# State updates and scores of spans 6 to 10 on quarters of the array, and another issue order for spans 0 to 9

## The chip, the cores and the metric

The kernel runs on one core of a Trainium2 chip. The metric is device time in microseconds (us) of one execution. The core has TensorE (PE in the profile; its weight loads are listed apart as PEld), VectorE (DVE), ScalarE (ACT), GpSimd (POOL) and SyncE (SP), which here only issues DMAs. Each engine works through its own queue in order and waits for others by semaphores.

## The reference, cut to what matters

A gated linear recurrence per head, then a feed-forward layer with ELU:

```python
def _attn_ref(q, k, v, alpha):            # (4, 8, 768, 48) each
    for t in range(S):
        state = alpha[:, :, t, :, None] * state + einsum('bhd,bhe->bhde', k[:, :, t], v[:, :, t])
        y[:, :, t] = einsum('bhd,bhde->bhe', q[:, :, t], state)
...
def _moe_ref(x, w_in, w_out):             # x: 3072 x 384, w_in: 384 x 2048, w_out: 2048 x 384
    h = x @ w_in
    g = where(h > 0, h, exp(minimum(h, 0)) - 1)
    return g @ w_out
```

x is y with the heads side by side. The result is wanted in near float32 accuracy, so each operand of the large products is split into a high and a low fp32r part and three products are summed.

## The kernel before

**Recurrence.** The sequence of each of the four batches is cut into six spans (the code's windows) of 128 steps, 24 in all, numbered i; a span has two chunks of 64 steps. Eight heads lie on the partitions in two halves (48 rows of each 64), four times along the free axis. A span passes these steps, each named by one or two letters in the code:

- L (LA, LB): load of q, k and alpha; LV: load of v in its two layouts into one of four buffers vs. V0 (lines 181 to 183) loads for spans 6 to 9 a second copy of the first half of v, whose other half stays zero.
- SC: running product P of alpha (L192). LN, EX, KA, KB, KC: the decay factors and the scaled k (L201 to L224). SQ: q times P into the tile st (L235, L238); ZS (L245) zeroes the other half of st for spans 6 to 10.
- TP and KN: transposes of k by PE and a copy by ACT, in spans 0 to 5; TA and TB: 32 by 32 transposes by DVE, from span 6 on.
- S: scores on PE; MK: their mask on DVE (L335, L330).
- U: products of k and v on PE; UA, UB, UC (L381, L410, L412): the states after each chunk. UP corrects U of span 1 on PE.
- YL, Y3 and Y: output of the span on PE; XH and XL: its high and low part in x; XP: the low part on PE for spans 0 and 1; XD: a small DMA that brings heads 6 and 7 to their rows of x.

S and U come in two forms. Before span QS (scores) or QU (updates), S (L318) and U (L362) use all 128 rows of the array, against zeros in one half, and 64 or 48 of its columns, and write one PSUM bank. From there on, S4 (L303) and U4 (L346) go round the four 64 by 64 quarters of the array:

```python
QU, QS, SHARE = 10, 11, 11
...
    QUADS = ((0, 0), (1, 1), (0, 1), (1, 0))
...
            for a, c in QUADS:
                r, cs = slice(64 * a, 64 * a + D), slice(c * C, (c + 1) * C)
```

and write two banks; from span SHARE on, the scores of a span use the banks that the updates of the span before left. Both forms have 16 matmuls (32 passes, as they are float32). The mask in the first form is two DVE instructions of 64 x 512, in the second four of 64 x 256 (QUADS again).

**Feed-forward.** x is worked in 12 blocks of 256 tokens (b), d_ff in 8 groups of 256 (j). A.b.j: h from x and w_in, 18 matmuls (L625); RA, RB, RC: the ELU on ACT, ACT and DVE; GH and GL: its high and low part (ACT, DVE); O.b.j: 12 matmuls into two PSUM banks (L676); Z.b: store.

**Weights.** They come as pairs of 32-bit words and are rebuilt on the chip: F loads one of 16 pieces, DA, DB, DC (DVE, L551 to L563) rebuild two pieces at a time, WH (ACT, L589) makes the high part, WL (L609) the low part, on DVE for the pieces in WLV and on POOL for the others. WP makes the low parts of pieces 0 and 2 on PE. KAV, KBV and SQV say in the same way for which spans KA, KB and SQ run on DVE rather than on POOL.

**Order.** START lists the steps of spans 0 to 9 and of the first 25 A.b.j, with the weights, in the order of issue; each engine gets its instructions in that order. After it, a loop (`steady`) places the steps by fixed distances. PSUM has eight banks under one tag; a new tile takes a bank that was released earlier in the program. X.2 in START are two matmuls on constants whose result nobody reads, and 12 of them (WARM) stand ahead of it.

Of the kernel before, what the change touches and what calls it, by code (L numbers as in the profile page):

```python
# [42 lines left out]


START = """
LA.0 SC.0 X.2 LB.0 LN.0 EX.0 LA.1 SQ.0 LB.1 KA.0 KB.0 SC.1 SQ.1 F.0 F.2 KC.0 LN.1 EX.1 LV.1 KA.1 LV.0 S.0 KB.1
TP.0 KC.1 L.2 PC.0 TP.1 KN.1 KN.0 L.3 PC.1 DA.0 DB.0 S.1 DC.0 U.0 WH.0 U.1 UC.0 X.2 UA.0 UP.1 SC.2 WP.0 F.6
WH.2 LN.2 SQ.2 MK.1 F.4 LV.3 F.1 UC.1 SC.3 UA.1 EX.2 MK.0 WP.2 DA.2 F.3 YL.1 KA.2 L.5 YL.0 LV.2 KB.2 KC.2 F.9
LN.3 Y3.1 Y.1 EX.3 DB.2 Y3.0 KA.3 PC.2 KB.3 Y.0 WL.0 XH.1 LC.0 S.2 F.11 TP.2 XP.1 XH.0 KN.2 XP.0 SQ.3 KC.3
DC.2 TP.3 DA.1 U.2 XL.1 KN.3 U.3 DB.1 WL.2 DC.1 WH.4 UB.2 XL.0 F.5 S.3 L.4 PC.3 A.0.0 UA.2 WH.6 WH.1 UC.2 F.10  # L50
A.0.1 CA.0 WL.6 A.0.3 MK.2 UB.3 UA.3 WH.3 MK.3 UC.3 WL.4 RA.0.0 YL.2 F.7 LV.5 RB.0.0 YL.3 RA.0.1 Y3.2 SC.4
WL.1 Y3.3 F.12 SC.5 SQ.4 DA.3 WL.3 LN.5 Y.2 LN.4 RB.0.1 SQ.5 F.8 Y.3 RC.0.0 EX.4 EX.5 F.14 A.0.2 RC.0.1 XH.3
XH.2 L.7 XL.3 XL.2 GH.0.0 GH.0.1 KA.4 GL.0.0 DA.5 DB.3 KA.5 KB.5 DC.3 CB.0 LV.7 V0.7 LV.6 V0.6 RA.0.2 RA.0.3
A.1.0 RB.0.2 LV.4 UB.6 A.1.3 KC.5 A.1.1 RC.0.2 GL.0.1 TP.5 RB.0.3 WH.7 RA.1.3 GH.0.2 RC.0.3 S.5 DA.4 RA.1.0
RB.1.3 WL.7 GL.0.2 WH.5 KN.5 DB.5 A.1.2 RB.1.0 O.0.0 MK.5 RC.1.3 DB.4 GH.0.3 WL.5 O.0.1 RA.1.2 O.0.2 LC.1
RC.1.0 KB.4 GL.0.3 L.6 RA.1.1 KC.4 DC.4 TP.4 RB.1.1 KN.4 DC.5 GH.1.0 WH.8 GL.1.0 O.0.3 U.4 GH.1.3 PC.5 GL.1.3
WL.8 RB.1.2 RC.1.1 WH.11 GH.1.1 DA.6 GL.1.1 S.4 A.0.4 RC.1.2 O.1.0 WH.10 MK.4 DB.6 GH.1.2 GL.1.2 RA.0.4 WL.11
PC.4 UB.4 WL.10 O.1.1 RB.0.4 WH.9 DC.6 O.1.2 A.0.5 WL.9 WH.12 U.5 F.15 UC.4 UB.1 UA.4 F.13 RC.0.4 Y.4 UA.5
WH.14 RA.0.5 GH.0.4 RB.0.5 GL.0.4 WL.12 CA.1 SC.6 LN.6 SC.7 WL.14 O.1.3 RC.0.5 DA.7 A.0.7 L.8 A.0.6 LN.7 DB.7
GH.0.5 RA.0.7 GL.0.5 DC.7 EX.6 KA.6 XH.4 O.0.4 RB.0.7 XL.4 RA.0.6 WH.13 RB.0.6 WL.13 A.1.4 RC.0.7 A.1.5 O.0.5  # L60
EX.7 WH.15 KB.6 GH.0.7 KA.7 RC.0.6 KB.7 GH.0.6 RA.1.4 GL.0.7 UB.0 RA.1.5 LV.8 Y.5 GL.0.6 A.1.6 CB.1 KC.6
RB.1.5 XD.4 WL.15 RB.1.4 XH.5 O.0.6 TB.6 RC.1.5 SQ.6 ZS.6 ZV.6 O.0.7 SQ.7 ZS.7 RA.1.6 RC.1.4 GH.1.4 XL.5
GH.1.5 GL.1.4 RB.1.6 XD.5 TA.6 GL.1.5 A.2.3 Z.0 RA.2.3 RC.1.6 U.6 V0.8 KC.7 GH.1.6 S.6 S.7 TA.7 RB.2.3 RC.2.3
O.1.4 GL.1.6 A.1.7 A.2.4 LC.2 MK.6 PC.6 A.2.2 UA.6 UC.6 SC.8 RA.1.7 RB.1.7 TB.7 GH.2.3 LN.8 O.1.5 Y.6 EX.8
RC.1.7 SQ.8 ZS.8 KA.8 GH.1.7 L.10 MK.7 RA.2.2 U.7 KB.8 GL.1.7 O.1.6 RB.2.2 A.2.0 KC.8 LV.9 V0.9 UB.7 UC.7 PC.7
TA.8 UA.7 L.9 RC.2.2 XH.6 LV.10 RA.2.0 RB.2.0 O.1.7 RC.2.0 A.2.1 Z.1 SC.9 GH.2.0 RA.2.1 TB.8 XL.6 A.2.7 RA.2.4
GL.2.0 RB.2.1 Y.7 GL.2.3 RC.2.1 LN.9 U.8 RB.2.4 GH.2.2 EX.9 S.8 MK.8 SQ.9 ZS.9 XH.7 A.2.6 XD.6 XL.7 O.2.0
RA.2.7 KA.9 RB.2.7 GH.2.1 GL.2.2 RC.2.4 A.2.5 RC.2.7 UB.8 GL.2.1 PC.8 RA.2.6 RB.2.6 UC.8 O.2.1 RA.2.5 SC.10
UA.8 KB.9 XD.7 RB.2.5 O.2.2 LN.10 A.3.0 O.2.3 GH.2.4 LV.11 RC.2.5 RC.2.6 GH.2.7 L.11 KC.9 RA.3.0 TB.9 EX.10
GH.2.5 RB.3.0 GL.2.4 O.2.4 KA.10 SQ.10 ZS.10 KB.10 GH.2.6 GL.2.5 KC.10 GL.2.7 GL.2.6 TA.9 RC.3.0 O.2.5 TB.10  # L70
TA.10 O.2.6 PC.9 S.9 GH.3.0 MK.9 GL.3.0
"""
# [896 lines left out]
```

## Time and profile before

| | us |
|---|---|
| median of 3 runs | 513.34 (511.15 to 514.16) |
| profiled execution | 510.82 |
| its span | 509.1 |
| outside the span | 1.7 |
| busy: PE | 499.0 (98%) |
| busy: DVE | 394.3 (77%) |
| busy: ACT | 301.5 (59%) |
| busy: POOL | 123.2 (24%) |

Busy is the time in which an engine had an instruction running; idle time of an engine is listed with what ended it. The timeline merges instructions of one line in a row: start, busy time, line, shapes and how many. Matmuls overlap, so the duration of a group runs a little past the start of the next; from the start of one group to that of the next is what the group took on PE. The scan of SC is printed as TENSOR_TENSOR_SCAN in the trace and as SCALAR_TENSOR_TENSOR in listings of the order.

### The profile page before, as it was taken

To read this page: it belongs to the slowest core of one execution; us is meant where nothing else is said; L and a number is where in the kernel's file an instruction comes from. 1 tells how busy PE (TensorE), PEld (TensorE's weight loads), DVE (VectorE), ACT (ScalarE), POOL (GpSimd) and SP (SyncE) were. 2 spreads that over 40 slices of the span, in tenths; PEclk is the share of its full clock that TensorE was granted. 3 is DMA by queue.
4 is the path that set the end of the run, shared out by engine and by line. 5 is a ranking of instruction groups with operands and counts; after the bars stand their busy time and mean duration, and the time that the engine had idled before them with its cause. 6 is when DMAs were issued, how large, how long until landed. Compare 5 with 4: busy or idle time off the path is not lost.

```text
span 509.1 us, 13170 instructions
## 1 busy us (share of the span) xinstructions
PE 499.0 (98%) x5404; PEld 482.5 (95%) x5404; DVE 394.3 (77%) x801; ACT 301.5 (59%) x689; POOL 123.2 (24%) x115
## 2 busy tenths in 40 slices
PE   6999999999999999999999999999999999999996
PEld 3789999999999999999999999999999999999995
DVE  7898998998999788788888888788888887333431
ACT  3576566644653657667667667666666665564442
POOL 3233631643420304303303304303213110000000
PEclk9999999999999999999999999999999999999999
DMA  8999605032330442432532523524524221210001
GB/s 311 403 410 382 188 1 215 13 120 76 119 102 1 133 148 54 158 121 77 164 102 94 165 79 117 164 72 124 160 74 127 71 66 37 72 40 1 31 4 36
DMA packets 22724, 61.53 MB, mean 121 GB/s; under 512 B 2944, under 2 KB 10112, under 8 KB 22656
## 3 DMA queue, kind: packets, MB, share of 16 engines
q1 hardware_dynamic: 22368, 60.22, 36.0%
q8 instruction: 44, 0.72, 0.6%
q10 hardware_dynamic: 288, 0.39, 0.2%
q14 instruction: 24, 0.20, 0.1%
HBM read 53.92 MB, written 4.72 MB: 115 GB/s over the span
## 4 chain that ended last, share of the span: by engine, by line
PE 95%; DMA 3%; SPq 1%; issue 1%; DVE 0%; ACT 0%
PE h L625 41%; PE o L676 40%; PE y L428 4%; DMA vs<-in_vv_dram 3%; PE sc L318 2%; PE q L346 2%; PE u L362 1%; PE y L423 1%; PE q L303 1%; PE wp L112 1%; PE tp L259 0%; SPq L535 0%; PE y L467 0%; PE yl L423 0%; SPq L174 0%
## 5 line engine op out<-in xcount | busy, mean ns | idle before, releaser
L625 PE MATMUL h<-xt,w 128*128 128x256 f32 x1728 | 221.4, 282 | 0.0
L625 PEld LDWEIGHTS h<-xt,w 128*128 128x128 f32 x1728 | 214.0, 188 | 1.5
L676 PE MATMUL o<-w,gh 128*128 128x384 f32 x768 | 198.4, 339 | 0.0
L676 PEld LDWEIGHTS o<-w,gh 128*128 128x128 f32 x768 | 135.6, 188 | 0.2
L676 PE MATMUL o<-w,gl 128*128 128x384 f32 x384 | 129.9, 338 | 0.0
L649 ACT CAST gh<-h 128x512 fp32r<-128x512 f32 x96 | 56.3, 587 | 88.3 <-DVE h L643 71.7
L643 DVE SCALAR_TENSOR_TENSOR h<-r,h 128x512 f32<-128x512 f32 x96 | 66.1, 693 | 51.1 <-ACT r L638 50.5
L633 ACT ACTIVATE r<-h 128x512 f32<-128x512 f32 x96 | 56.7, 594 | 75.1 <-PE h L625 73.5
L238 POOL TENSOR_TENSOR st<-qka,P 64x512 f32<-64x512 f32 x36 | 42.9, 1190 | 212.0 <-issue 166.5
L662 DVE TENSOR_TENSOR gl<-h,gh 128x512 fp32r<-128x512 f32 x96 | 66.1, 690 | 34.2 <-ACT gh L649 33.0
L269 DVE STREAM_TRANSPOSE kn<-qka 32x128 f32<-32x128 f32 x288 | 87.1, 302 | 4.1
L676 PEld LDWEIGHTS o<-w,gl 128*128 128x128 f32 x384 | 72.1, 188 | 0.0
L638 ACT ACTIVATE r<-r 128x512 f32<-128x512 f32 x96 | 60.5, 633 | 2.5
L192 DVE TENSOR_TENSOR_SCAN P<-qka,first 128x516 f32<-128x516 f32 x24 | 29.6, 1237 | 2.3 <-DMA qka<-in_qka_dram 1.5
L214 POOL TENSOR_TENSOR qka<-qka,R 128x512 f32<-128x512 f32 x18 | 23.9, 1330 | 12.5 <-ACT R L206 12.4
L219 POOL TENSOR_TENSOR R<-P,R 128x512 f32<-128x512 f32 x19 | 24.7, 1300 | 5.0 <-DVE qka L214 3.9
L330 DVE TENSOR_TENSOR st<-q,mask 64x256 f32<-64x256 f32 x52 | 22.0, 422 | 1.0
L428 PEld LDWEIGHTS y<-st,vs 128*64 128x64 f32 x576 | 18.3, 138 | 4.2 <-issue 4.0
L581 ACT ACTIVATE ck<-ck,lim 128x384 f32<-128x384 f32 x32 | 20.9, 653 | 1.0
L428 PE MATMUL y<-st,vs 128*64 128x64 f32 x576 | 20.7, 225 | 0.0
L201 ACT ACTIVATE R<-P 128x512 f32<-128x512 f32 x24 | 15.1, 633 | 8.4 <-DVE P L192 8.4
L576 ACT ACTIVATE ck<-ck 128x384 f32<-128x384 f32 x32 | 18.2, 568 | 0.1
(105 smaller groups left out, 418.5 us busy)
## 6 DMA issues: line engine op xcount, KB each, us to landing
qka<-in_qka_dram SPq DMA_DIRECT2D x22, 770.0 KB, 5.1
raw<-in_wgt_dram SPq DMA_DIRECT2D x16, 768.0 KB, 11.2
ck<-in_wgt_dram SPq DMA_DIRECT2D x32, 384.0 KB, 3.1
vs<-in_vv_dram SPq DMA_DIRECT2D x36, 192.0 KB, 5.3
out_dram<-ot SPq DMA_DIRECT2D x22, 192.0 KB, 2.0
vs<-in_vv_dram SPq DMA_DIRECT2D x6, 384.0 KB, 9.3
xt<-y SPq DMA_DIRECT2D x40, 48.0 KB, 2.3
qka<-in_qka_dram SPq DMA_DIRECT2D x2, 512.0 KB, 4.8
```

Of the source, the lines that this page charges most:

```text
L192: nc.vector.tensor_tensor_scan(out=P.rearrange("p n w -> p (n w)"), data0=t[:, 2 * NP * W:], data1=first.rearrange("p n w -> p (n w)"), in ...
L219: eng(KBV, i).tensor_tensor(out=d["R"], in0=pw(i), in1=d["R"], op=ALU.mult)
L238: eng(SQV, i).tensor_tensor(out=st[r, a], in0=d["q"][r], in1=pw(i)[r], op=ALU.mult)
L269: nc.vector.transpose(out=kn[32 * t:32 * t + 32, :, 32 * g:32 * g + 32], in_=d["kt"][32 * g:32 * g + 32, :, 32 * t:32 * t + 32])
L428: nc.tensor.matmul(out[64 * a:64 * a + m], lhsT=lhs(i, c, a)[:, n * D:n * D + m], rhs=d["st"][:, a, n, c * C:(c + 1) * C], start=start, st ...
L625: nc.tensor.matmul(h[:, f, :], lhsT=t[:, wi, ws], rhs=x[:, c, xi, :], start=(f == 0 and k == 0), stop=(k == 8), skip_group_check=True)
L633: nc.scalar.activation(out=r, in_=d["h"], func=AF.Relu, scale=-1.0)
L638: nc.scalar.activation(out=d["r"], in_=d["r"], func=AF.Exp, scale=-1.0)
L643: nc.vector.scalar_tensor_tensor(out=d["h"], in0=d["r"], scalar=-1.0, in1=d["h"], op0=ALU.add, op1=ALU.max)
L649: nc.scalar.copy(out=gh, in_=d["h"])
L662: nc.vector.tensor_tensor(out=gl, in0=d["h"], in1=d["gh"].bitcast(F32), op=ALU.subtract)
L676: nc.tensor.matmul(o[:, 0:DM], lhsT=gt[:, f, ms], rhs=t[:, wi, f * DM:f * DM + DM], start=(j == 0 and f == 0 and k == 0), stop=(j == NJ - ...
```

## The change

QU and QS go to 6, so that spans 6 to 10 use the quarters as well (updates of 6 to 9, scores of 6 to 10). With this V0 and ZS do nothing and are no longer in START, UB and UC of span 6 take the form of the later spans, and each U and each S of these spans holds two banks rather than one (SHARE stays 11). The lists that say what runs on DVE change, and START is another order. The steady part changes only in U of span 9, S of span 10, and what hangs on them.

```diff
-QU, QS, SHARE = 10, 11, 11
+QU, QS, SHARE = 6, 6, 11
 
-WLV, KAV, KBV, SQV = (1, 3, 9, 10, 12), (0, 1, 3, 6, 7, 10), (0, 1, 2, 3, 8), (1, 3, 4, 5)
+WLV, KAV, KBV, SQV = (0, 4), (0, 1, 2, 3, 10), (0, 3, 5, 6), (1, 2, 3, 5)
...
-LA.0 SC.0 X.2 LB.0 LN.0 EX.0 LA.1 SQ.0 LB.1 KA.0 KB.0 SC.1 SQ.1 F.0 F.2 KC.0 LN.1 EX.1 LV.1 KA.1 LV.0 S.0 KB.1
...
+LA.0 LB.0 SC.0 LN.0 EX.0 LA.1 KA.0 KB.0 LB.1 SC.1 X.2 LV.0 LN.1 X.2 KC.0 F.2 SQ.0 EX.1 F.0 TP.0 KN.0 S.0 U.0
...
```

What the first lines move on PE, from the last matmul on constants ahead of the first span: wp is the constants' bank, sc the scores, tp the transposes, u the updates, yl and y the outputs, wd the weights' low part. Before:

```order
L112 MATMUL wp<-first 128x512
L318 MATMUL sc<-st,qka 64x64 x16
L259 MATMUL tp<-ident,qka 128x128 x8
L318 MATMUL sc<-st,qka 64x64 x16
L362 MATMUL u<-vs_105,kn 64x48 x16
L362 MATMUL u<-vs_106,kn 64x48 x16
L112 LDWEIGHTS first
L112 MATMUL wp<-first 128x512
L112 LDWEIGHTS first
L112 MATMUL wp<-first 128x512
L388 MATMUL u<-vs_106,minus 128x192 x2
L598 MATMUL wd<-wm,ident 128x384
```

After, on PE, the same place (all line numbers are one lower):

```order
L111 MATMUL wp<-first 128x512
L258 MATMUL tp<-ident,qka 128x128 x4
L317 MATMUL sc<-st,qka 64x64 x16
L361 MATMUL u<-vs_105,kn 64x48 x16
L422 MATMUL yl<-st,vs_105 64x64 x6
L258 MATMUL tp<-ident,qka 128x128 x4
L466 MATMUL y<-y_219,sel 64x128 x6
L422 MATMUL y<-st,vs_105 48x64 x18
L317 MATMUL sc<-st,qka 64x64 x16
L361 MATMUL u<-vs_106,kn 64x48 x16
L387 MATMUL u<-vs_106,minus 128x192 x2
L485 MATMUL y<-xt,minus 128x384
```

Span 0 now runs through to its output before span 1, whose scores and updates stood ahead of it, and the two later matmuls on constants have gone ahead of all spans.

On DVE, from the scan of span 0 on (P is the running product, qka holds k, R the decay factors, wm the rebuilt weights), before:

```order
L192 SCALAR_TENSOR_TENSOR P<-qka,first 128x516
L214 TENSOR_TENSOR qka<-qka,R 128x512
L219 TENSOR_TENSOR R<-P,R 128x512
L192 SCALAR_TENSOR_TENSOR P<-qka,first 128x516
L235 TENSOR_TENSOR st<-qka,P 128x512
L224 SCALAR_TENSOR_TENSOR qka<-R,qka 128x512
L214 TENSOR_TENSOR qka<-qka,R 128x512
L219 TENSOR_TENSOR R<-P,R 128x512
L224 SCALAR_TENSOR_TENSOR qka<-R,qka 128x512
L551 TENSOR_SCALAR wm<-raw_146 128x1536
```

and after:

```order
L191 SCALAR_TENSOR_TENSOR P<-qka,first 128x516
L213 TENSOR_TENSOR qka<-qka,R 128x512
L218 TENSOR_TENSOR R<-P,R 128x512
L191 SCALAR_TENSOR_TENSOR P<-qka,first 128x516
L223 SCALAR_TENSOR_TENSOR qka<-R,qka 128x512
L234 TENSOR_TENSOR st<-qka,P 128x512
L213 TENSOR_TENSOR qka<-qka,R 128x512
L334 TENSOR_TENSOR st<-sc,mask 128x2x4x64
L223 SCALAR_TENSOR_TENSOR qka<-R,qka 128x512
L411 SCALAR_TENSOR_TENSOR vs_106<-u,P 128x192
L550 TENSOR_SCALAR wm<-raw_148 128x1536
```

KC of span 0 now stands ahead of SQ of span 1, and the mask and the new state of span 0 ahead of the first weights.

On PE, where START ends and the steady part begins (S.9, Y.8, U.9, S.10, A.3.1; q is a bank of the quarters), before:

```order
L318 MATMUL sc<-st,qka 64x64 x16
L428 MATMUL y<-st,vs_105 64x64 x16
L362 MATMUL u<-vs_106,kn 48x48 x8
L362 MATMUL u<-v_114,kn 48x48 x8
L318 MATMUL sc<-st,qka 64x64 x16
L625 MATMUL h<-xt,w_233 128x256 x18
```

and after:

```order
L302 MATMUL q<-st,qka 64x64 x16
L427 MATMUL y<-st,vs_105 64x64 x16
L345 MATMUL q<-vs_106,kn 64x48 x16
L302 MATMUL q<-st,qka 64x64 x16
L624 MATMUL h<-xt,w_310 128x256 x18
```

The steps stand in the same row, in the other form, and between them hold six banks rather than three, beside the one of y.

## Rows read from the trace of the kernel before

**Rows 1.** Windows: start:end, length, busy time (instructions) per engine, clock, DMA share, GB/s
```profile
7.80:10.30 2.50, 0.01 (x1) 0.01 (x1) 2.38 (x3) 1.34 (x4) 0.00 (x0) 1.00 1.01 420
...
11.00:14.40 3.40, 3.40 (x42) 2.95 (x41) 3.30 (x5) 0.41 (x1) 0.00 (x0) 0.55 1.03 418
...
34.00:181.00 147.00, 147.00 (x1658) 143.86 (x1660) 131.42 (x236) 83.93 (x185) 56.19 (x45) 1.00 0.40 131
```

**Rows 2.** Waits of PE, whole span: us in total, times, longest
```profile
PE sc L318 <- issue: 2.5, 1, 2.5
...
PE u L362 <- DMA vs<-in_vv_dram: 0.4, 1, 0.4
```

**Rows 3.** Timeline of PE, U and S of span 8, first form
```profile
136.06 0.53 PE L362 MATMUL u<-vs,kn 128*48 128x48 f32 x16
...
136.78 1.12 PE L318 MATMUL sc<-st,qka 128*64 128x64 f32 x32
137.82 1.44 PE L625 MATMUL h<-xt,w 128*128 128x256 f32 x10
```

**Rows 4.** Timeline of PE, U of span 10 and S of span 11, quarters
```profile
181.24 0.68 PE L346 MATMUL q<-vs,kn 64*64 64x48 f32 x32
181.74 0.66 PE L303 MATMUL q<-st,qka 48*64 48x64 f32 x32
182.33 1.34 PE L625 MATMUL h<-xt,w 128*128 128x256 f32 x9
```

**Rows 5.** Groups by line and shape: busy us, mean ns, idle before
```profile
L330 DVE TENSOR_TENSOR st<-q,mask 64x256 f32<-64x256 f32 x52 | 22.0, 422 | 1.0
...
L381 DVE TENSOR_TENSOR q<-vs,q 48x192 f32<-48x192 f32 x22 | 7.9, 359 | 0.4
...
L609 POOL TENSOR_TENSOR w<-wm,w 128x768 fp32r<-128x768 f32 x5 | 11.0, 2202 | 26.2 <-ACT w L589 26.2
...
L335 DVE TENSOR_TENSOR st<-sc,mask 64x512 f32<-64x512 f32 x10 | 6.9, 689 | 1.0 <-PE sc L318 0.8
...
L245 POOL MEMSET st<- 64x512 f32 x10 | 5.2, 524 | 0.3
...
L609 DVE TENSOR_TENSOR w<-spare,w 128x768 fp32r<-128x768 f32 x4 | 3.8, 947 | 0.0
```

**Rows 6.** Timeline of DVE, SQ of span 1 and KC of span 0
```profile
8.92 0.69 DVE L235 TENSOR_TENSOR st<-qka,P 128x512 f32<-128x512 f32 x1
9.53 0.68 DVE L224 SCALAR_TENSOR_TENSOR qka<-R,qka 128x512 f32<-128x512 f32 x1
```

**Rows 7.** Timeline of PE, from the first scores to the first A
```profile
10.32 1.73 PE L318 MATMUL sc<-st,qka 48*64 48x64 f32 x32 [2.51 <-issue]
11.98 1.97 PE L259 MATMUL tp<-ident,qka 128*128 128x128 f32 x8
13.88 1.22 PE L318 MATMUL sc<-st,qka 48*64 48x64 f32 x32
...
17.52 0.60 PE L112 MATMUL wp<-first 128*128 128x512 bf16 x2
17.96 0.81 PE L388 MATMUL u<-vs,minus 128*128 128x192 f32 x4
...
28.32 0.66 PE L259 MATMUL tp<-ident,qka 128*128 128x128 f32 x4
28.74 0.60 PE L486 MATMUL y<-xt,minus 128*128 128x384 f32 x2
29.17 0.60 PE L259 MATMUL tp<-ident,qka 128*128 128x128 f32 x4
30.19 2.69 PE L362 MATMUL u<-vs,kn 128*64 128x48 f32 x61 [0.42 <-DMA vs<-in_vv_dram]
...
33.82 2.38 PE L625 MATMUL h<-xt,w 128*128 128x256 f32 x18
```

**Rows 8.** Timeline of ACT, UA of span 0
```profile
17.71 0.32 ACT L379 ACTIVATE vs<-u 128x192 f32<-128x192 f32 x1
```

More of the change, by code (lines that the diff above doesn't have):

```diff
@@ L32 @@
 WARM = 12
-QU, QS, SHARE = 10, 11, 11
-WLV, KAV, KBV, SQV = (1, 3, 9, 10, 12), (0, 1, 3, 6, 7, 10), (0, 1, 2, 3, 8), (1, 3, 4, 5)
+QU, QS, SHARE = 6, 6, 11
+WLV, KAV, KBV, SQV = (0, 4), (0, 1, 2, 3, 10), (0, 3, 5, 6), (1, 2, 3, 5)
 WPE, XPE, GPE, UPE = (0, 2), (0, 1), (), (1,)
 START = """
-LA.0 SC.0 X.2 LB.0 LN.0 EX.0 LA.1 SQ.0 LB.1 KA.0 KB.0 SC.1 SQ.1 F.0 F.2 KC.0 LN.1 EX.1 LV.1 KA.1 LV.0 S.0 KB.1
-TP.0 KC.1 L.2 PC.0 TP.1 KN.1 KN.0 L.3 PC.1 DA.0 DB.0 S.1 DC.0 U.0 WH.0 U.1 UC.0 X.2 UA.0 UP.1 SC.2 WP.0 F.6
@@ L48 @@
[L48 to L71, printed above, removed]
+LA.0 LB.0 SC.0 LN.0 EX.0 LA.1 KA.0 KB.0 LB.1 SC.1 X.2 LV.0 LN.1 X.2 KC.0 F.2 SQ.0 EX.1 F.0 TP.0 KN.0 S.0 U.0
+SQ.1 UA.0 KA.1 KB.1 MK.0 L.2 KC.1 UC.0 YL.0 LV.1 TP.1 PC.0 Y3.0 Y.0 KN.1 DA.0 PC.1 LV.2 DB.0 L.3 F.4 S.1 SC.2
@@ new lines @@
+U.1 XH.0 F.6 DC.0 UP.1 LN.2 XP.0 EX.2 KA.2 SQ.2 MK.1 UA.1 F.5 WH.0 WP.0 YL.1 F.1 F.3 UC.1 Y3.1 KB.2 SC.3 KC.2
+WH.2 XL.0 PC.2 LN.3 DA.2 EX.3 SQ.3 Y.1 DB.2 KA.3 XH.1 TP.2 WP.2 DC.2 KB.3 KN.2 DA.1 DB.1 XP.1 KC.3 U.2 XL.1
+WL.2 LC.0 WL.0 S.2 A.0.0 RA.0.0 WH.6 WL.6 F.7 A.0.1 MK.2 UB.2 UA.2 TP.3 LV.3 UC.2 S.3 L.4 KN.3 F.9 YL.2 U.3
+WH.4 SC.4 WL.4 Y3.2 Y.2 UA.3 PC.3 RB.0.0 MK.3 XH.2 DA.3 SQ.4 DC.1 DB.3 YL.3 LN.4 XL.2 Y3.3 UB.3 A.0.2 LV.4
+WH.3 EX.4 F.10 CA.0 F.8 WL.3 Y.3 A.0.3 XH.3 UC.3 DC.3 XL.3 L.5 F.12 RA.0.1 KA.4 KB.4 A.1.1 A.1.0 LV.5 F.11
@@ new lines @@
+RC.0.0 RB.0.1 RC.0.1 WH.7 GH.0.0 SC.5 DA.5 RA.0.2 GH.0.1 A.1.2 RB.0.2 DB.5 RA.1.0 KC.4 RC.0.2 WH.1 RB.1.0 F.14
+GH.0.2 GL.0.0 RC.1.0 WL.1 RA.1.1 GL.0.2 A.1.3 RA.0.3 GL.0.1 RB.0.3 TP.4 UB.0 DA.4 PC.4 RB.1.1 WL.7 WH.5 KN.4
+O.0.0 RC.0.3 O.0.1 GH.0.3 DB.4 U.4 WL.5 GL.0.3 RC.1.1 DC.4 RA.1.3 GH.1.1 S.4 LN.5 O.0.2 O.0.3 RB.1.3 DC.5 LV.6
+L.6 WH.8 MK.4 UB.4 RA.1.2 EX.5 LV.7 GH.1.0 UA.4 RB.1.2 WL.8 GL.1.0 WH.9 KA.5 RC.1.2 CB.0 A.0.4 GH.1.2 GL.1.1
+UC.4 WH.10 KB.5 RA.0.4 KC.5 O.1.0 RC.1.3 TP.5 GL.1.2 SQ.5 GH.1.3 LC.1 DA.6 CA.1 KN.5 WH.11 L.7 O.1.1 DB.6
@@ new lines @@
+RB.0.4 WL.10 U.5 PC.5 RC.0.4 GL.1.3 GH.0.4 UA.5 A.1.4 A.0.5 SC.6 RA.1.4 WL.11 LN.6 EX.6 KA.6 WL.9 DC.6 F.15
+RB.1.4 RA.0.5 O.1.2 GL.0.4 WH.14 O.1.3 RC.1.4 RB.0.5 RC.0.5 GH.0.5 GH.1.4 S.5 KB.6 SC.7 KC.6 WH.12 Y.4 O.0.4
+WL.12 GL.1.4 PC.6 LN.7 EX.7 WL.14 MK.5 GL.0.5 F.13 A.0.6 TB.6 A.0.7 CB.1 L.8 RA.0.6 A.1.5 DA.7 KA.7 TA.6 DB.7
+O.0.5 XH.4 RB.0.6 RA.0.7 ZV.6 RC.0.6 RA.1.5 O.1.4 GH.0.6 XL.4 RB.0.7 Y.5 RB.1.5 KB.7 DC.7 KC.7 GL.0.6 A.1.6
+WH.13 WL.13 TB.7 SQ.7 XH.5 WH.15 PC.7 XL.5 RC.0.7 RC.1.5 GH.0.7 LV.8 O.0.6 GL.0.7 TA.7 XD.4 WL.15 RA.1.6 SQ.6
@@ new lines @@
+RB.1.6 U.6 O.0.7 UA.6 XD.5 UB.6 UB.1 RC.1.6 GH.1.5 A.1.7 Z.0 GL.1.5 UC.6 GH.1.6 U.7 S.6 UA.7 O.1.5 SC.8 UB.7
+MK.6 RA.1.7 LN.8 UC.7 A.2.4 RB.1.7 RA.2.4 GL.1.6 S.7 A.2.1 EX.8 MK.7 A.2.0 RC.1.7 Y.6 RB.2.4 RC.2.4 KA.8
+RA.2.1 RB.2.1 Y.7 GH.1.7 RA.2.0 KB.8 KC.8 RB.2.0 RC.2.1 GL.1.7 L.9 SC.9 SQ.9 XH.6 XH.7 RC.2.0 GH.2.0 A.2.3
+O.1.6 LN.9 TB.8 XL.7 O.1.7 A.2.5 RA.2.3 LV.10 EX.9 SQ.8 TA.8 GL.2.0 L.10 GH.2.1 KA.9 GL.2.1 U.8 PC.8 XL.6 Z.1
+UA.8 S.8 XD.7 RA.2.5 A.2.2 RB.2.3 UB.8 A.2.6 UC.8 RC.2.3 KB.9 MK.8 KC.9 O.2.0 RA.2.2 RB.2.2 GH.2.4 RC.2.2 TA.9
@@ L72 @@
+SC.10 GH.2.2 RB.2.5 XD.6 LN.10 A.2.7 GL.2.2 GL.2.4 RA.2.6 RB.2.6 EX.10 O.2.1 RC.2.6 KA.10 GH.2.3 A.3.0 RC.2.5
+RA.2.7 GL.2.3 L.11 O.2.2 LC.2 PC.9 LV.11 KB.10 RA.3.0 TB.9 O.2.3 RB.3.0 KC.10 GH.2.5 RB.2.7 GL.2.5 GH.2.6
+O.2.4 RC.2.7 O.2.5 GH.2.7 RC.3.0 GL.2.6 GH.3.0 O.2.6 TA.10 S.9 GL.2.7 GL.3.0 SQ.10 LV.9 MK.9 TB.10
 """
```

## The prediction

> **What bounds the kernel now.** I read the windows first, then what PE waited for, then the timeline of PE stage by stage. From 34 to 181 us, which is nearly all that START orders, PE is busy in 147.00 of 147.00 us at the full clock, and DVE in 131.42 [rows 1]. A busy PE can hide waits, so I also looked through its starts there, and found the A and O of START spaced as those of the steady part. Only two PE waits on the whole span matter, 2.5 and 0.4 us, and both stand before the first A at 33.82 us [rows 2, 7]. So time is the work of PE, plus what is lost ahead of the first A. The reader is to see in rows 7 that this head is not dense: PE is idle from 7.80 to 10.30 [rows 1], and after it the granted clock is 0.55 from 11.0 to 14.4 us, so for most of that stretch it is the lower level (1.2 GHz). DVE is no bound, but with 15.6 us free in 147 it is the next.
>
> **Quarters.** In the first form U took 136.78 - 136.06 = 0.72 us and S 137.82 - 136.78 = 1.04 us in span 8 [rows 3], and the other first-form groups of spans 6 to 10 look alike. On quarters U took 181.74 - 181.24 = 0.50 and S 182.33 - 181.74 = 0.59 us, both with 32 passes [rows 4]. Four updates (spans 6 to 9) save 4 x 0.22 = 0.9 us and five scores (6 to 10) save 5 x 0.45 = 2.25 us: 3.1 us, all on PE, the path that sets the end. The durations include whatever PE needs to turn from one form to the other, since they run from start to start. In the new order two of the groups stand alone among large matmuls, not beside each other; that costs at most the difference of S and U on quarters, 0.09 us each, so I keep 2.9 to 3.3 as bounds and take 3.1.
>
> A rule speaks against this part. The Trainium skill (TensorEngine Tiling (Array Packing), Tiling Modes) says that a change of the tiling mode, not just of the tile, drains TensorE. The rows above hold the drains already, and the first form is tiled too (128 by 48 and 128 by 64), so by the rule the number of mode changes hardly moves and the sum stays as it is.
>
> **Off PE.** DVE loses four WL (0.947 each, 3.8 us; of the two pieces left in WLV, piece 0 is made on PE anyway), one KA and one KB of 128 x 512 (some 0.69 each, as the SQ of that size), 1.4 us. It gains masks, 5 x (4 x 0.422 - 2 x 0.689) = 1.6 us, and UB of span 6, 2 x 0.359 = 0.7 us [rows 5, 6]. That is 2.9 us less, so DVE falls about as much as PE, and the margin between them stays. POOL loses ten memsets (5.2 us) and gains four WL of 2.2 us (8.8) and a KA and a KB, each between 0.69 and 2.2 us: 5 to 8 us more, on 56.19 busy of 147 [rows 1, 5]. Queued behind a WL on POOL are the next KA, KB and SQ, and for these the transposes and S on PE wait; a late WL delays them by 2.2 us at most, and the profile lists POOL as waiting for ACT ahead of WL, not as waited for. I cost it at nothing; if that cover is gone, it costs one such 2.2 us. The second v copies were small loads after 40 us and saved DMA time is worth nothing there: DMA share is 0.40 [rows 1].
>
> **The head.** Three things are gained.
> First, the start: the first PE step needs KC of span 0, which stood behind SQ of span 1 on DVE. It moves up by 9.53 - 8.92 = 0.61 us [rows 6].
> Second, the pair of matmuls on constants that took 17.96 - 17.52 = 0.44 us in dense time goes to where PE was idle [rows 1, 7].
> Third, the v of span 2 is now loaded ahead of most weights. Before it, PE's transposes took 30.19 - 29.17 = 1.02 us to the next start against 28.74 - 28.32 = 0.42 without a wait: 0.60 us of waiting for that DMA [rows 7].
> Sum 1.65 us.
>
> Two things are lost, because span 0 now runs through alone. U, then UA on ACT, then YL follow each other on PE with nothing between: 0.32 us [rows 8] and two handovers of about 0.1 us (KC ends at 10.21, S starts at 10.32 [rows 6, 7]), so 0.5 us. YL of span 1, its copy on ACT and Y also follow directly: another 0.4 us by the same row. Neither is in the trace of before, so they are estimates; the bounds are 0 (hidden by matmuls still running) and twice the sum, 1.8 us, if DA to DC, which now stand behind the new state of span 0 on DVE, bring the first weights late as well. I take 0.9, as one handover row carries it.
> The low clock cost before: S took 11.98 - 10.32 = 1.66 us against 1.04, and eight transposes 1.90 against 2 x 0.42: 1.7 us in all [rows 3, 7]. I leave it as it is: PE still idles after the constants. Net gain of the head 1.65 - 0.9 = 0.8 us, bounds -0.2 and, with the clock up, 0.8 + 1.7 = 2.5.
>
> **The sum.** 3.1 + 0.8 = 3.9 us off the profiled 510.82: 506.9. The median of the runs is 2.5 us above the profiled execution, so 513.34 - 3.9 = 509.4 is my forecast for the median. About 0.5% (2.6 us) is what a measurement of this kernel can tell from no change; its three runs spread by 0.6%.
>
> **Rivals.**
> (a) The clock stays up. PE now idles from about 8.2 to 9.7 us rather than from 7.8 to 10.3; if the clock is not taken back, 1.7 us more return: 507.7. For it speaks the shorter idle stretch; against it that PE is idle in half of it still.
> (b) Only the quarters pay. The serial start of span 0, or a DVE that comes late for the outputs of spans 2 and 3 (it must finish their low parts before the first A of block 1), gives the head's gain back and up to 1.8 us more: 510.2 to 513, say 511. For it: DVE was busy in 3.30 of 3.40 us of the head's middle [rows 1]. Against: by then PE has more A queued than it had.
> (c) Banks, the slower end. Each U and each S of spans 6 to 10 holds two of eight banks. In the last rows of START and the first steady ones, q banks and the o banks leave one or two for h, where there were three or more. A bank comes back only after GL on DVE, which now may stand behind four masks of 0.422 us. If PE waits for these 1.7 us in each of five spans, that is 8.5 us against 3.9 gained: 517.9. It decides from where PE has less queued than one mask of DVE; from about 2.3 spans on of the five it ends slower than before. Against it: spans 11 on run the four masks without a PE wait [rows 2], though with shared banks.
> (d) A quarter form in START that is no faster than the full one, since it writes two fresh banks: only the head counts, 512.5. The banks are fresh in span 10's updates too, which took 0.50 [rows 4].
> (e) Four at once. If four quarters worked at the same time, U would take 0.72/4 = 0.18 and S 1.04/4 = 0.26 us, saving 4 x 0.54 + 5 x 0.78 = 6.1 instead of 3.1 us: 506.4. The Trainium skill (TensorEngine Tiling (Array Packing), Theoretical Speedup) gives up to 2 times for one small dimension and more where both are small. The rows of span 10 and 11 give 1.4 and 1.8 times, so the trace bears out little of it.
>
> **How the numbers follow.** Forecast 0.45 (508.4 to 510.6); (a) 0.15; (b) 0.22; (c) 0.10; (d) 0.04; (e) 0.04. Faster by over 0.5% is below 510.8: 0.40 of the forecast, (a), (e) and 0.04 of (b), 0.63. Slower is (c) but for its mildest case, and a tail of (b): 0.10. The rest, 0.27, is no change. The range reaches from a little below (e) and (a), 505.8, to the end of (b), 512.8; it leaves out (c) and the tails.
>
> **What would show it.** In the new trace S and U of spans 6 to 10 run as L302 and L345 at 0.59 and 0.50 us; other values touch the first term. The first transposes start at 9.7 us, and the first A at about 30.2: 33.82 less 0.8, and less 2.8 for TP, S and U of span 3, which now come after it (0.42, 1.04, and half of what is left of 33.82 - 30.19 without an S, 1.3) [rows 3, 7]. A clock row at full level from 11 to 14.4 us is (a). PE waits between 34 and 181 us, or stretched A with DVE dense beside them, are (b) or (c), and their place tells which: before 60 us (b), behind 100 us (c). I am wrong if such waits sum to over 3 us.

## The result, and the profile after

| | us |
|---|---|
| kernel before, median of 4 runs | 512.25 (510.83 to 514.16) |
| kernel after, median of 4 runs | 506.26 (505.86 to 506.90) |
| ratio | 0.987, interval 0.984 to 0.990 |
| profiled execution, before and after | 510.82 and 506.90 |
| span of it | 509.1 and 505.2 |

The change is faster by 6.0 us. The forecast was 3.9 us, from a median of before of 513.34; a fourth run has brought that median to 512.25. The time lies inside the range (505.8 to 512.8), but at its low end and outside the likeliest case's own range (508.4 to 510.6). Between the two profiled executions the difference is 3.92 us, the size of the forecast sum. So the question is why the medians lie 2 us farther apart than the profiles.

Windows of the kernel after (start:end, length, busy time and instructions of PE, PEld, DVE, ACT, POOL, then PE's clock, DMA share, GB/s):

```profile
7.80:10.30 2.50, 0.56 (x5) 0.43 (x5) 2.42 (x3) 1.18 (x3) 0.00 (x0) 1.00 1.00 412
11.00:14.40 3.40, 3.03 (x70) 2.54 (x68) 2.39 (x5) 1.34 (x5) 1.18 (x1) 1.00 1.02 420
...
34.00:181.00 147.00, 146.78 (x1776) 142.34 (x1775) 133.00 (x251) 88.42 (x196) 60.65 (x41) 1.00 0.39 130
```

The second row is the one to compare with [rows 1]: the clock was 0.55 there and is 1.00 now, with 70 matmuls where there were 42. From 34 to 181 us PE is as full as it was, but for 0.2 us.

What PE waited for in the kernel after (us in total, times, longest):

```profile
PE tp L258 <- issue: 2.3, 1, 2.3
PE wp L111 <- DVE first L105: 2.1, 1, 2.1
PE yl L422 <- ACT vs L378: 0.4, 1, 0.4
PE y L466 <- ACT y L455: 0.4, 1, 0.4
PE wd L597 <- DVE wm L562: 0.2, 1, 0.2
PE sc L317 <- DVE gl L661: 0.2, 1, 0.2
```

The wait for the DMA of v [rows 2] is gone. The waits for ACT and for the weights are new: span 0 and then span 1 run through alone, as the prediction said.

Timeline of PE in the head of the kernel after (start, busy time, line, operation, shapes, how many, and in brackets the wait ahead of it):

```profile
9.74 0.63 PE L258 MATMUL tp<-ident,qka 128*128 128x128 f32 x4 [2.26 <-issue]
10.30 1.15 PE L317 MATMUL sc<-st,qka 48*64 48x64 f32 x32
...
13.14 0.46 PE L422 MATMUL yl<-st,vs 48*64 48x64 f32 x8 [0.37 <-ACT vs L378]
13.53 0.66 PE L258 MATMUL tp<-ident,qka 128*128 128x128 f32 x4
...
19.57 0.88 PE L597 MATMUL wd<-wm,ident 128*128 128x384 f32 x2 [0.24 <-DVE wm L562]
...
22.62 0.88 PE L466 MATMUL y<-y,sel 128*64 128x128 f32 x12 [0.35 <-ACT y L455]
...
29.50 4.54 PE L624 MATMUL h<-xt,w 128*128 128x256 f32 x36
33.87 0.60 PE L258 MATMUL tp<-ident,qka 128*128 128x128 f32 x4
34.40 1.15 PE L317 MATMUL sc<-st,qka 48*64 48x64 f32 x32
35.38 0.68 PE L422 MATMUL yl<-st,vs 48*64 48x64 f32 x16
35.99 1.27 PE L361 MATMUL u<-vs,kn 128*64 128x48 f32 x32
37.19 0.88 PE L466 MATMUL y<-y,sel 128*64 128x128 f32 x12
```

The first A starts at 29.50. The transposes, S and U of span 3, which stood ahead of it, follow later and take (34.40 - 33.87) + (35.38 - 34.40) + (37.19 - 35.99) = 2.71 us. Against 33.82 [rows 7] the head is 33.82 - 29.50 - 2.71 = 1.6 us shorter.

Timeline of PE in the kernel after, quarters of spans 6 to 8:

```profile
105.75 0.68 PE L345 MATMUL q<-vs,kn 64*64 64x48 f32 x32
106.37 0.62 PE L675 MATMUL o<-w,gh 128*128 128x384 f32 x2
...
132.09 0.68 PE L345 MATMUL q<-vs,kn 64*64 64x48 f32 x32
132.59 0.66 PE L302 MATMUL q<-st,qka 48*64 48x64 f32 x32
133.18 4.49 PE L624 MATMUL h<-xt,w 128*128 128x256 f32 x36
```

U takes 0.50 and S 0.59 us in span 8, where they follow each other, as in [rows 4]; U of span 6, which stands alone between large matmuls, takes 0.62.

The last updates of the program, timeline of PE in the kernel before:

```profile
433.58 0.67 PE L346 MATMUL q<-vs,kn 64*64 64x48 f32 x16
```

The same updates in the kernel after:

```profile
430.14 0.67 PE L345 MATMUL q<-vs,kn 64*64 64x48 f32 x16
```

PE comes 3.44 us earlier there; the other 0.5 us of the 3.92 arise behind the last matmul and are no part of the change.

### The profile page after: what moved, and what is told of

Its sections match the earlier page's. It is cut to its first block, busy times and chain, and to the rows that moved or that the text cites. A ratio compares the mean times of both kernels' runs of the same rounds, so it can differ in the third digit from the quotient of the medians.

```text
span 505.2 us, 13182 instructions
## 1 busy us (share of the span) xinstructions
PE 495.1 (98%) x5404; PEld 477.7 (95%) x5404; DVE 392.8 (78%) x807; ACT 302.5 (60%) x689; POOL 128.2 (25%) x111
## 4 chain that ended last, share of the span: by engine, by line
PE 88%; DMA 7%; DVE 2%; issue 1%; ACT 0%; SPq 0%
PE o L675 40%; PE h L624 38%; DMA raw<-in_wgt_dram 4%; PE y L427 4%; DMA qka<-in_qka_dram 3%; PE q L345 2%; PE q L302 2%; PE wp L111 1%; PE y L422 1%; PE sc L317 1%; DVE spare L550 1%; DVE gl L661 1%; DVE P L191 0%; DVE spare L556 0%; DVE h L642 0%
## 5 line engine op out<-in xcount | busy, mean ns | idle before, releaser
L329 DVE TENSOR_TENSOR st<-q,mask 64x256 f32<-64x256 f32 x72 | 30.4, 422 | 2.7 <-PE q L302 1.3
L213 POOL TENSOR_TENSOR qka<-qka,R 128x512 f32<-128x512 f32 x19 | 26.1, 1374 | 17.7 <-DVE gl L661 10.4
L608 POOL TENSOR_TENSOR w<-spare,w 128x768 fp32r<-128x768 f32 x7 | 15.7, 2245 | 28.2 <-ACT w L588 16.5
## 6 DMA issues: line engine op xcount, KB each, us to landing
raw<-in_wgt_dram SPq DMA_DIRECT2D x16, 768.0 KB, 12.6
qka<-in_qka_dram SPq DMA_DIRECT2D x2, 512.0 KB, 5.3
```

What stands on the lines that cost most here:

```text
L329: nc.vector.tensor_tensor(out=d["st"][r, a, :, c * C:(c + 1) * C], in0=d["s4"][a][o], in1=mask[o].unsqueeze(1).broadcast_to([64, NP, C]), ...
```

## The experiments

Two theories were to be told apart. **The sum was right and the clock was left out:** the quarters and the order bring about the 3.9 us; the rest is TensorE's clock in the head, which in most runs of before falls for longer than in the profiled one, and after the change stays up. **Its rival:** quarters or head bring more than the sum gave them, and the clock has little to do with it.

**The kernel before, twelve runs more.** Nothing is edited; the runs show what the clock does to the time.

> The kernel before, unchanged, for the clock and the time of each run. Clock theory: its runs lie 1 to 3 us above the profiled 510.82 because the granted clock falls in the head, for a stretch that differs from run to run; time and mean clock go together, some 0.5 us for each 0.001 of mean clock (half of the time at the lower level), from about 0.999 at 510.8 to about 0.993 at 514. Rival (the scatter is of the loads): times scatter as much, but at one and the same mean clock of 0.997.

Measured: 511.07 us (510.66 to 515.60). Its profiled execution (510.89) in windows:

```profile
7.80:9.60 1.80, 0.00 (x0) 0.00 (x0) 1.76 (x3) 0.65 (x2) 0.00 (x0) 1.00 0.99 406
9.60:16.40 6.80, 6.09 (x80) 5.55 (x81) 6.54 (x8) 3.06 (x8) 0.00 (x0) 0.50 0.98 382
```

The lower level lasts 6.8 us here, not the 3.4 of [rows 1], and the time is the same within 0.1 us. With the runs of before that went with the other experiments there are 91, and each has its mean granted clock:

| mean clock of the run | runs | median us | from, to |
|---|---|---|---|
| 0.994 to 0.998 | 25 | 511.29 | 510.27, 513.15 |
| 0.991 to 0.993 | 27 | 511.09 | 510.66, 512.33 |
| 0.988 to 0.990 | 21 | 513.08 | 512.67, 514.70 |
| up to 0.987 | 18 | 514.37 | 513.78, 517.51 |

None is at 0.999 or 1.000. The time does go with the clock, but not in proportion, which is what I had expected: the runs at 0.991 and above have nearly the same median, and those below lie 2 to 3 us above it in the median, up to 6 in single runs. (The mean alone is no price: one run reads 0.939 and takes 513.78.) No profile of before itself shows a run of the lower rows; two of its variants below do. The profile that the prediction rests on is one of the mild runs.

**The order of after without the quarters.** This measures the two parts of the change apart. (The other half, quarters in the old order, was not run: counting the banks that are live in that order, A.2.4 would need eleven of the eight.)

```diff
-QU, QS, SHARE = 6, 6, 11
+QU, QS, SHARE = 10, 11, 11
...
-RB.1.3 DC.5 LV.6
+RB.1.3 DC.5 LV.6 V0.6
...
```

(V0 of spans 7 to 9 and ZS of spans 6 to 10 come back in the same way.)

> The new order and lists, with the first form of updates and scores (QU 10, QS 11, second v copies and the zeroing put back). Theory that quarters are worth 3.1 us and the rest is the head: 506.26 + 3.1 = 509.4 (508.9 to 510.0), scatter under 1.5 us and clock 0.999 or more as in the kernel after, since its head is the same. Rival that the quarters give about 5 us and the order 1: 511 to 512.

Measured: 509.82 us (509.39 to 511.54), ratio 0.994 (0.992 to 0.996), all six runs at 0.997 or above. The slowest, 511.54, is the profiled one; it carries a late DVE step that is told below. Timeline of PE in it, U and S of span 8:

```profile
135.09 0.56 PE L361 MATMUL u<-vs,kn 128*48 128x48 f32 x16
135.48 0.53 PE L361 MATMUL u<-v,kn 128*48 128x48 f32 x16
135.84 1.12 PE L317 MATMUL sc<-st,qka 128*64 128x64 f32 x32
136.89 3.32 PE L624 MATMUL h<-xt,w 128*128 128x256 f32 x26
```

From start to start, the four U take 3.07 us here and 2.12 in the kernel after, the five S 5.20 and 3.03: 3.12 us on the traces, 509.82 - 506.26 = 3.6 between the medians. The forecast was 3.1. The rest of the 3.6 is not placed; it is less than the intervals of the two ratios leave open. So the quarters are what was forecast within these intervals, and the order brings the other 2.4 us of the 6.0.

**Both pairs of constants early, in before.** Does their new place keep the clock up?

```diff
-LA.0 SC.0 X.2 LB.0 LN.0 EX.0
+LA.0 SC.0 X.2 X.2 LB.0 LN.0 EX.0
...
-U.1 UC.0 X.2 UA.0 UP.1
+U.1 UC.0 UA.0 UP.1
```

> The kernel before with one edit: the second pair of matmuls on constants goes ahead of the first scores, to the other pair. Clock theory: PE's idle stretch shrinks from 2.5 to 2.1 us, the clock stays up, and the 0.44 us of the pair, the 1.7 us of the profiled execution and the scatter go: 508.5 to 510, scatter under 1.5 us, clock 0.999. If the idle stretch is still too long for that: 511.8, the 0.44 us alone, clock and scatter as before.

Measured: 511.28 us (509.92 to 514.27), ratio 0.999 (0.997 to 1.001); five of twelve runs at 0.990 or below take 512.5 to 514.3. In its profile the clock still reads 0.51 from 10.3 to 13.8 us. That move alone does nothing.

**After, without its constants.** The opposite edit.

```diff
-LB.1 SC.1 X.2 LV.0 LN.1 X.2 KC.0 F.2 SQ.0
+LB.1 SC.1 LV.0 LN.1 KC.0 F.2 SQ.0
```

> The kernel after without its two pairs of matmuls on constants behind the first 12 (their result is read by nobody): PE idles from about 7.0 to 9.7 us. Clock theory: the clock falls as in the kernel before, 507.5 to 509.5, scatter of 2 to 3 us, mean clock 0.997 or less. Rival that constants and clock have nothing to do with it: 506.3 within 0.5 us, clock 1.000.

Measured: 510.36 us (509.20 to 511.56), ratio 0.995 (0.993 to 0.998), all ten runs at 0.987 to 0.992. Window of its profile:

```profile
11.00:17.60 6.60, 6.34 (x79) 5.16 (x78) 4.99 (x6) 2.41 (x7) 1.18 (x1) 0.50 1.02 418
```

Its first transposes and its first A in the timeline of PE:

```profile
9.54 0.63 PE L258 MATMUL tp<-ident,qka 128*128 128x128 f32 x4 [2.15 <-issue]
...
31.92 1.33 PE L624 MATMUL h<-xt,w 128*128 128x256 f32 x9
```

The two pairs are 0.9 us of work whose result nobody reads, and without them the kernel is 4.1 us slower, more than I expected. Its first transposes even start earlier than after's (9.54 against 9.74), and its first A 2.4 us later (31.92 against 29.50). So in after's order the fall of the clock is on the path.

**Before, with the idle stretch filled.** Ten more constants ahead of the first scores.

```diff
-LA.0 SC.0 X.2 LB.0 LN.0 EX.0
+LA.0 SC.0 X.12 LB.0 LN.0 EX.0
```

> The kernel before with one edit: ten more matmuls on constants (X.12 for the first X.2), so that PE has work in its idle stretch from 7.8 to about 10. Clock theory: no lower clock in any run (mean 0.999 or more), the scatter of 510.4 to 517.5 shrinks to under 1.5 us, and the median is the profiled 510.82 less the 1.7 us that the lower clock cost there: 509.1 (508.6 to 509.6). Then the low clock cost the median run of before some 2 to 3 us. Rival (the clock falls for another reason, or the head is bound by loads and loses nothing to it): median 511 to 512.5 and scatter as before.

Measured: 511.28 us (509.90 to 513.72), ratio 0.999 (0.996 to 1.001). Nine runs at 0.997 or above (509.90 to 511.85, median 510.6), three at 0.988 or 0.989 (513.6 to 513.7). A window of its profile:

```profile
11.00:14.40 3.40, 2.74 (x56) 2.16 (x51) 3.32 (x4) 1.23 (x3) 0.00 (x0) 1.00 1.05 427
```

Three rows of PE's timeline in it:

```profile
12.48 0.66 PE L259 MATMUL tp<-ident,qka 128*128 128x128 f32 x4 [0.48 <-DVE qka L224]
...
30.05 2.40 PE L362 MATMUL u<-vs,kn 128*64 128x48 f32 x61 [0.40 <-DMA vs<-in_vv_dram]
...
33.39 0.87 PE L625 MATMUL h<-xt,w 128*128 128x256 f32 x5
```

The clock is up, and still the first A comes at 33.39, only 0.43 us earlier than in [rows 7]: PE now waits for DVE and for v. I had expected 509.1. So this row prices rival (a) of the prediction: on before's order, full clock is worth 0.4 us against the profiled run, not 1.7, but 2 to 7 us against the runs below 0.991, which that profile is not. It also gives before's time at the full clock, about 510.6, though these nine runs still spread by 2 us.

**Before, with KC of span 0 ahead of SQ of span 1** and four constants at the start.

```diff
-LA.0 SC.0 X.2 LB.0
+LA.0 SC.0 X.4 LB.0
...
-SC.1 SQ.1 F.0 F.2 KC.0 LN.1
+SC.1 KC.0 SQ.1 F.0 F.2 LN.1
...
-U.1 UC.0 X.2 UA.0 UP.1
+U.1 UC.0 UA.0 UP.1
```

> The kernel before with the first edits of the new order alone: all constants first (as tried before), and KC of span 0 ahead of SQ of span 1 on DVE, so that PE starts its first scores 0.6 us earlier, at 9.7. Theory that the shorter idle stretch keeps the clock up: clock 0.999 or more in most runs, median 508.0 to 508.8 (510.82 less 1.7, 0.44 and 0.6 at most), little scatter. Rival, that the kind of work behind the idle stretch matters or that 1.9 us idle are still too many: clock 0.997 or less in most runs, 510 to 511.5.

Measured: 511.52 us (509.79 to 514.80), ratio 0.998 (0.995 to 1.001). Six runs at 0.997 or above take 509.8 to 510.9, six at 0.992 or below 512.1 to 514.8. Window of its profile, one of the latter:

```profile
13.20:23.40 10.20, 10.20 (x109) 8.48 (x108) 8.54 (x9) 5.35 (x12) 1.72 (x2) 0.50 1.02 413
```

The clock falls for 10.2 us, later than in [rows 1] and for longer; half the runs pay for a fall, and the median is on the rival's side. The first A in the same profile:

```profile
36.72 1.45 PE L625 MATMUL h<-xt,w 128*128 128x256 f32 x10
```

It comes 2.9 us later than in [rows 7], and the run (513.38) takes 2.6 us more than that profile's: the long fall is paid ahead of the first A.

**After, with SQ of span 1 ahead of KC of span 0 again.**

```diff
-LN.1 X.2 KC.0 F.2 SQ.0 EX.1 F.0 TP.0 KN.0 S.0 U.0
-SQ.1 UA.0
+LN.1 X.2 SQ.1 KC.0 F.2 SQ.0 EX.1 F.0 TP.0 KN.0 S.0 U.0
+UA.0
```

> The kernel after with one edit undone: SQ of span 1 again ahead of KC of span 0 on DVE, so that PE starts 0.6 us later. If the length of the idle stretch decides the clock: it falls in most runs (0.997 or less) and the median rises by 0.6 and 1.5 to 4 us, to 508.4 to 511. If the clock stays up all the same: 506.3 to 506.9, as the 0.6 us are the whole of it.

Measured: 510.28 us (507.07 to 511.92), ratio 0.995 (0.992 to 0.998). Four runs at 0.998 or above take 507.07 to 507.54, eight at 0.988 to 0.992 take 509.96 to 511.92. Window of its profile (511.42), one of the eight:

```profile
11.00:21.10 10.10, 9.84 (x139) 8.66 (x141) 7.01 (x8) 3.28 (x9) 1.19 (x1) 0.50 1.02 413
```

The first A in its timeline of PE:

```profile
34.25 1.93 PE L624 MATMUL h<-xt,w 128*128 128x256 f32 x14
```

This separates the two effects of one 0.69 us instruction. With the clock up the kernel is about 1 us slower than after; the late start alone, 10.37 for the first transposes against 9.74, is the 0.6 us that the prediction counted for it. With the clock down it is 4 to 6 us slower.

**After, with the transposes and S of span 1 between the serial steps of span 0.** Can the new waits of 0.4 us be filled?

```diff
-MK.0 L.2 KC.1 UC.0 YL.0 LV.1 TP.1 PC.0 Y3.0 Y.0 KN.1 DA.0 PC.1 LV.2 DB.0 L.3 F.4 S.1 SC.2
+MK.0 L.2 KC.1 UC.0 TP.1 YL.0 LV.1 PC.0 Y3.0 S.1 Y.0 KN.1 DA.0 PC.1 LV.2 DB.0 L.3 F.4 SC.2
```

> The kernel after with two steps moved on PE: the transposes of span 1 ahead of YL of span 0, and the scores of span 1 between YL and Y of span 0, so that something stands in the two serial handovers of span 0. By the waits of the kernel after (0.37 us of YL for UA) it gains 0.4 us: 505.9, clock 1.000. If the mask and the weights that follow on DVE then come later by as much: 506.3, no difference that shows.

Measured: 507.05 us (506.85 to 509.50), ratio 0.990 (0.987 to 0.994). The wait of YL goes and one of 0.6 us of the transposes for KC of span 1 on DVE takes its place; the first A starts at 29.81. No gain: the four runs at 1.000 take 506.85 to 507.16, more than after.

**After again.** Nothing is edited.

> The kernel after, unchanged, for the share of its runs in which the clock falls. Theory: it has no lower-clock stretch ahead of the end in most runs, and these lie at 506.2 (505.8 to 506.9); a run with a stretch at the lower clock (mean clock 0.992 or less) lies 2.5 to 5 us higher, as in the two variants of it with 0.992. With at least two of three runs undisturbed the median is 506.3. Rival, that the four runs seen so far were luck: half of the runs at 0.992 or less and a median of 508 or more.

Measured: 506.31 us (506.06 to 509.20), ratio 0.988 (0.985 to 0.992). Of the ten runs of after, nine are at 0.999 or 1.000 (505.86 to 506.90) and one at 0.992 (509.20). So the clock can still fall, but rarely does; it cost 3 us in that run.

**Before, filled, with v of span 2 loaded early.** Does that load hold the head at the full clock?

```diff
-LA.0 SC.0 X.2 LB.0
+LA.0 SC.0 X.12 LB.0
...
-TP.0 KC.1 L.2 PC.0 TP.1 KN.1 KN.0 L.3
+TP.0 KC.1 L.2 LV.2 PC.0 TP.1 KN.1 KN.0 L.3
...
-YL.0 LV.2 KB.2 KC.2
+YL.0 KB.2 KC.2
```

> The kernel before with the idle stretch filled (X.12 for the first X.2), and v of span 2 loaded ahead of the loads that wait for buffers (LV.2 ahead of L.3). Theory that the head of the kernel before is bound by this load, so that what the clock gives back is lost again in front of the updates of span 2: that wait goes, the first A starts at 32.4 rather than 33.4 us, and the undisturbed runs fall from 510.2 to about 509.2. Rival (another load or DVE is late by as much): first A at 33.0 or later, undisturbed runs at 510 or more.

Measured: 511.75 us (510.32 to 514.31), ratio 0.999 (0.996 to 1.001). Its six runs at 0.995 or above take 510.32 to 512.32, no less than with the filling alone. No wait for v is left in its profile, though the clock is low there from 12.6 to 22.8, which would hide one; its first A starts at 37.50, 4.1 us later than in the filled kernel, and the run (514.31) takes 4.1 us more. That load alone is not what holds before's head; the theory fell.

**After, with the rest of its idle stretch filled.**

```diff
-LV.0 LN.1 X.2 KC.0
+LV.0 LN.1 X.7 KC.0
```

> The kernel after with five more matmuls on constants (X.7 for the second X.2), so that PE is busy nearly until its first transposes at 9.7 us. Theory: nothing changes in undisturbed runs, 506.2, and fewer runs show the lower clock, none of 0.992 or less; median 506.2. Rival: constants run late when the clock rises late, the first transposes come after 10 us, and the median is 506.8 or more.

Measured: 506.50 us (506.07 to 510.17), ratio 0.987 (0.984 to 0.990): no better than after, which loses nothing to the clock in most runs. The run of 510.17 is the profiled one, and it seems to show how a chance delay grows. Two windows of it:

```profile
55.00:58.00 3.00, 1.23 (x9) 0.79 (x8) 3.00 (x6) 1.77 (x4) 2.12 (x1) 1.00 0.06 23
58.00:61.50 3.50, 3.50 (x12) 3.50 (x13) 3.50 (x4) 2.88 (x6) 1.02 (x1) 0.51 0.00 0
```

Two rows of its timeline of PE:

```profile
56.70 0.66 PE L258 MATMUL tp<-ident,qka 128*128 128x128 f32 x4 [1.24 <-DVE gl L661]
57.90 0.89 PE L675 MATMUL o<-w,gh 128*128 128x384 f32 x2 [0.54 <-DVE gl L661]
```

One row of its timeline of DVE:

```profile
50.44 0.96 DVE L550 TENSOR_SCALAR spare<-raw 128x1536 int32<-128x1536 int32 x1 [1.29 <-issue]
```

DVE starts one weight step 1.29 us late, waiting for nothing that the profile shows (in the profile of after the same instruction starts at 49.20, without a wait). Five microseconds later PE waits for GL, and then the clock falls for 3.5 us. The profile of the order without the quarters has the same late step (1.20) and the same two waits, without the fall.

**After, with v of span 2 loaded late.**

```diff
-PC.1 LV.2 DB.0 L.3
+PC.1 DB.0 L.3
...
-YL.1 F.1 F.3 UC.1
+YL.1 F.1 F.3 LV.2 UC.1
```

> The kernel after with one load put back: v of span 2 behind six pieces of weights, about where the kernel before has it. By the bytes ahead of it, it lands at 27 to 29.5 us, and the updates of span 2 stand at 27.4: if the load is what bounds the head, they wait 0.5 to 2 us for it, the first A starts at 30 to 31.5 rather than 29.5, and the undisturbed runs rise to 506.7 to 508. If it lands in time: 506.2, first A at 29.5.

Measured: 509.89 us (507.84 to 512.04), ratio 0.994 (0.992 to 0.997). Timeline of PE in its profile (508.05):

```profile
27.23 0.33 PE L485 MATMUL y<-xt,minus 128*128 128x384 f32 x1
29.29 1.21 PE L361 MATMUL u<-vs,kn 128*64 128x48 f32 x29 [1.74 <-ACT w L606]
...
31.43 0.74 PE L624 MATMUL h<-xt,w 128*128 128x256 f32 x4
```

U of span 2 now waits 1.74 us (ACT is named, but its same instructions run at the same time in the kernel after, from 27.84 to 29.48, where U does not wait for them; the load that was moved is issued at 15.84 and lands 13.3 us later, at 29.1), and the first A is 1.9 us late. The four runs at 0.998 or 1.000, this profile among them, take 507.84 to 508.05, 1.7 us more than after; seven of the other eight have a lower clock (0.993 or below). So the same load that gave nothing in before's order is worth 1.7 us in after's, plus the clock.

## Why the prediction was right or wrong

**Quarters: right.** 3.1 forecast, 3.12 on the traces with the order held fixed, 3.6 between medians. S and U run at 0.59 and 0.50 us in pairs, and standing alone costs U 0.12 and S 0.03 us more, where at most 0.09 each was bounded. Rivals (d) and (e) fall: the fresh banks cost nothing, and the gain is 1.4 and 1.8 times, not 4. That (e)'s 506.4 is the number nearest to the measured 506.26 is chance.

**Banks, rival (c): wrong, as thought.** The last wait in the list above, 0.2 us, stands at 61 us, ahead of all quarters. The masks of the quarters on DVE, in the groups of the page of the kernel after:

```profile
L329 DVE TENSOR_TENSOR st<-q,mask 64x256 f32<-64x256 f32 x72 | 30.4, 422 | 2.7 <-PE q L302 1.3
```

They take 422 ns, as in [rows 5], and nothing waits for a bank that they hold. The Trainium skill (TensorEngine Tiling (Array Packing), PSUM Bottleneck) warns that tiling speeds up TensorE but not the emptying of PSUM, which may become the bound after a fourfold speedup; at the 1.4 and 1.8 times of this case it does not, with DVE busy in 133.00 of 147 us.

**Off PE: right where it matters, off in size.** POOL rose by 5.0 us (5 to 8 forecast). DVE fell by 1.5 us, not 2.9, and nothing came of it.

**Head: right in its steps.** The first transposes start at 9.74 (9.7 forecast) and the first A at 29.50 (30.2). The two serial waits cost 0.37 + 0.35 = 0.72 us (0.9 forecast), and a wait for the first weights, which the prediction had in its upper bound alone, 0.24 more. The head gains 1.6 us between the profiles, twice the forecast 0.8, the clock among it; against the filled kernel's 33.39, at the full clock, it gains 1.2. But some 1.3 us of head and quarters together (1.6 + 3.1 - 3.44) are lost again in START. One place is U of span 4, which takes 0.3 us more than its like, 0.2 of it the wait for GL; the rest is not placed. Rival (b) is right in this part, but too small to decide. (By its own terms it ends at 513.34 - 3.1 + 1.8 = 512.0, not at the 513 and the 512.8 that the prediction gives.) So it is luck that the two profiled executions differ by just the forecast 3.9 us: 1.6 and 3.1 won, 1.3 lost, and 0.5 that arise behind the last matmul.

**The clock: this is the step that failed.** The prediction said of the low clock "I leave it as it is: PE still idles after the constants". It did not fall: the clock reads 1.00 from 11.0 to 14.4 us, the sign that was named for rival (a), to which I gave 0.15. Nor is it the shorter idle stretch that was named for (a): PE was to idle for 1.5 us (8.2 to 9.7), and it idles for 2.26 against 2.51 before. And the price of the low clock was read from one execution. The 1.7 us there were mostly hidden by other waits (0.4 came back when the clock was kept up in before's order), while the runs below 0.991 lose 2 us and more, and the profile was not one of them. Where these microseconds are lost can be read from the profiles: in the six of before and its variants the first A starts between 33.39 and 37.50, while the time of the run behind it is 476.5 to 477.3 us in all of them; in after's order, leaving out the two with the late DVE step, the first A starts between 29.35 and 34.25, and 476.6 to 477.4 us follow. So what a fall of the clock in the head costs is lost ahead of the first A, and nothing of it comes back. The same step stands behind "the median of the runs is 2.5 us above the profiled execution", which I carried over to the kernel after as if it were a constant. It went with the clock, and with which three runs were drawn. After's median is 0.64 below its profiled run.

So the 6.0 us are made up like this. Quarters: 3.6 (509.82 to 506.26). Order at the full clock: 0.8 (510.6, from the filled kernel, to 509.82). The clock: 512.25 - 510.6 = 1.6; with other medians of before (511.1 to 512.7 in the batches) it would be 0.5 to 2.1, so this term changes with the runs that are drawn, and the one of the order, 0.8, is less than the spread of the runs that it is taken from. (The 91 runs of before have a median of 511.9 and the ten of after 506.3, which makes 5.6 in place of 6.0.)

**Not settled:** what the clock follows. No edit of before kept its clock up as reliably as after's (two places of the constants, ten more of them, the earlier KC, the earlier v), and undoing any of three things in after let it fall again in most runs (constants 10 of 10, KC 8 of 12, v of span 2 in 7 of 12). It is not the length of the idle stretch ahead of the first span alone. In after's order the clock stayed up behind 2.26 us of it (after) and 2.5 us (the order without the quarters, in its list of PE's waits), and fell behind 2.15 us (without the constants, row above) and 2.03 us (SQ of span 1 ahead, in its timeline of PE):

```profile
PE tp L258 <- issue: 2.5, 1, 2.5
```

```profile
10.37 0.63 PE L258 MATMUL tp<-ident,qka 128*128 128x128 f32 x4 [2.03 <-issue]
```

The start itself differs from execution to execution: the same 16 matmuls on constants take from 5.1 to 6.4 us in the profiles of after's order. No run tests what that does to a later fall.

The Trainium skill (TensorE: Matmul & The Clock Gate, Part 1) says that the lower clock is the default and that activity releases it. That agrees in direction with after and its runs without constants, less plainly with before: there the kernel with ten more constants still fell in three runs of twelve, and the one with four constants at the start and the earlier KC in six. Also open is what holds before's head at the full clock beside its v.
